# Alpha and phi laid out by partition; in batch 0 ScalarE makes the scales' diagonals and copies both heads' turned exponentials

## The chip, the cores and the metric

The kernel runs on one core of a Trainium2 chip. The metric is device time in microseconds (us) of one execution; lower is better. The core has five instruction streams that run beside each other and wait for one another through semaphores: TensorE (PE in the profile, with its weight loads as PEld), VectorE (DVE), ScalarE (ACT), GpSimd (POOL) and SyncE (SP), which here issues all the DMAs. Each stream works through its instructions strictly in the order in which they were written.

## The reference, cut to what matters

```python
q, k, v: (4, 8, 576, 64)          # batch, heads, positions, width of a head
x = attention(rotate(q), rotate(k), v)            # softmax over 576 keys
x = x.transpose(0, 2, 1, 3).reshape(2304, 512)
h = x @ w_in                                      # (512, 2048)
x = (max(h, 0) + alpha * min(h, 0)) @ w_out       # alpha: (2048,)
logits = x @ phi                                  # (512, 32)
d = softmax(logits, over tokens);  c = softmax(logits, over slots)
slot_input = d.T @ x                              # 32 slots, 4 for each of 8 experts
slot_out[e] = max(slot_input[e] @ w1[e], 0) @ w2[e]
return c @ slot_out                               # (2304, 512)
```

`moe_w_in` and `moe_w_out` arrive as 64-bit floats; the kernel takes each element's two 32-bit words apart itself.

## The kernel before

Attention is cut into 4 batches of 4 pairs of heads. A pair has five rows of query blocks (four of 128 positions for both heads, and a tail). For a row and a head, TensorE makes the scores `st` (L419 in batch 0, L432 in the later ones), VectorE takes the row's maximum (L437), ScalarE the exponentials `e` (L442), VectorE the sum's reciprocal (L449, L450), and GpSimd scales `e` by it (L474). In batch 0 TensorE then turns the scaled exponentials (L495, tile `pt`) and they are copied out of PSUM into `ET`: head 0's by ScalarE (L504), head 1's by VectorE (L506). In batches 1 to 3 the turning is done by VectorE and a way through DRAM instead. `ET` feeds the product with v (L574), which is evacuated into `xt`.

Before that, a pair's q and k are rotated: two multiplications (L322) and an addition (L330 in batch 0, L325 later), on VectorE for the first pair and on GpSimd for all others.

Beside batch 0 the weights are prepared, since the first projection (L735) needs them. `w_in` comes in 8 tiles of 1 MB (`wraw`, L621) and `w_out` transposed in 8 more. VectorE joins each tile's words to 32-bit floats (L643, L645, L647). For a tile of `w_in`, ScalarE and TensorE find its largest value (L655, L229), VectorE makes from it a scale that is a power of two (`sw`, L202 to L206), and GpSimd writes the scaled tile as 16-bit floats (L658). What that rounding left over goes into a second 16-bit tile, in two halves (`split`): GpSimd makes a 128 x 128 matrix with the scale on its diagonal (`dg`, L262), TensorE multiplies the tile by it and subtracts the 16-bit part (L268, L269), and ScalarE copies the rest out (L273). That is 16 halves, and there is one buffer for `dg`. The tiles of `w_out` go into a product with `phi` (L696, L705).

The order of the instructions on every engine is written by a planner (`Plan`): each step (`op`) names its engine, an assumed cost and a due time, and the planner lays the steps out by simulating the engines with these costs. Where a step's engine or cost changes, all that follows may be laid out otherwise. The inputs are prepared on the host by `kernel`: `form` names a function for each array that is laid out anew there.

`alpha` (2048 values) is loaded by L239 into `al`, 128 partitions x 16, and `phi` (512 x 32) by L240 into `phs`, 128 x 4 x 32. Both lie in DRAM in their own order, so `al` is read value by value and `phs` in runs of 32 values.

Of the kernel before, what the change touches and what calls it, by code (L numbers as in the profile page):

```python
# [14 lines left out]
AF = mybir.ActivationFunctionType  # L15
ALU = mybir.AluOpType
# [15 lines left out]
W0, W1, WD, WB, WS, ATT, LEADS, LAG, PRE, ORD = 1.0, 2.2, -6.0, 0.5, 1.0, 3.4, (0.0, 0.3, 0.6, 0.8), 6.0, 9.0, 1.0  # L32
# [130 lines left out]
def attn_moe_softmoe(ctx, tc, qx, kx, vx, w_in, w_out, alpha, phi, w1, w2, tab, msks, w_out_t, out):  # L163
    nc = tc.nc
# [71 lines left out]
        for z, i, d in (("k", 2, -30), ("q", 0, -28))}  # L236
    s_tabs = Slot("tabs")
    msk_op = op(DMA, 450, 15, lambda: nc.sync.dma_start(msk, msks))
    al_op = op(DMA, 900, -3, lambda: nc.sync.dma_start(al, alpha.rearrange("(c p) -> p c", p=128)))  # L239
    phs_op = op(DMA, 450, 9, lambda: nc.sync.dma_start(phs, phi.rearrange("(c p) s -> p c s", p=128)))  # L240
    sel_op = op(DVE, 200, 20, lambda: nc.vector.tensor_reduce(
        sel4[:, 0], idf[:].rearrange("p (g s) -> p s g", s=NS), axis=AX.X, op=ALU.add))
    sel_op = op(DVE, 200, 20, lambda: nc.vector.tensor_copy(
# [11 lines left out]
    def split(due, scale, src, dst, n, cls, dep, uses, after=None):  # L255

        s_d, s_p = Slot("dg"), Slot(cls)
        e = {}

        def diag():  # L260
            e["d"] = wst.tile([128, 128], F32, tag="dg", name="dg", bufs=1)
            nc.gpsimd.tensor_scalar(e["d"], idf, scale(), 1.0, ALU.mult, ALU.mult)  # L262

        def mults():
            ps = ps_m.tile([128, n], F32, tag=cls, name="rest")
            hi = dst(0)
            e["p"] = ps if len(hi.shape) == 2 else ps[:].rearrange("p (r a f) -> p r a f", r=hi.shape[1], a=hi.shape[2])
            nc.tensor.matmul(ps, e["d"], src(), start=True, stop=False)  # L268
            nc.tensor.matmul(ps, neg["t"], hi, start=False, stop=True)  # L269

        o = op(POOL, 470, due, diag, [dep, neg_op], takes=[s_d], uses=[s_d])
        o = op(PE, n * 2.1, due - ATT, mults, [o, dep, after], takes=[s_p], uses=[s_d, s_p] + uses)
        return op(ACT, 595, due, lambda: nc.scalar.activation(dst(1), e["p"], AF.Copy), [o, after], uses=[s_p] + uses)  # L273

# [120 lines left out]
    def row_events(b, p, s, n, pair):  # L395
# [4 lines left out]
        c = {}  # L400
# [69 lines left out]
        for h in heads:  # L470
            def norm(h=h):
                if tail:
                    nc.gpsimd.tensor_scalar(c["e"][:, 1, 0:64], c["e"][:, 0, 512:S], c["mm"][:, 6:7], 1.0, ALU.mult, ALU.mult)
                nc.gpsimd.tensor_scalar(c["e"][:, h], c["e"][:, h], c["mm"][:, 6 + h:7 + h], 1.0, ALU.mult, ALU.mult)  # L474

            o2 = op(POOL, 1200 if tail else 820, n + h + LEADS[1], norm, [o], uses=[s_mm, s_e])
            norms.append(o2)
            if moved:
                def block(h=h):
                    if h == 0:  # L480
                        c["tb"] = att.tile([128, 16, 2, 32], F32, tag="tb", name="tb", bufs=2)
                    nc.vector.transpose(  # L482
                        out=c["tb"][:, :, h].rearrange("p (q m) j -> p q m j", q=4),
                        in_=c["e"][:, h, 64 * h:64 * h + 512].rearrange("p (m q j) -> p q m j", m=4, q=4))

                blocks.append(op(DVE, 760, n + h + LEADS[2], block, [o2] + blocks[-1:], takes=[] if h else [s_tb], uses=[s_e, s_tb]))
                continue
            s_pm = Slot("pm")

            def turn(h=h):  # L490
                if h == 0 and first:
                    open_ET()
                c["pt", h] = ps_m.tile([128, 4, 128], F32, tag="pm", name="pt")
                for i in range(4):
                    nc.tensor.transpose(c["pt", h][:, i], c["e"][:, h, 64 * h + 128 * i:64 * h + 128 * i + 128], idf)  # L495

            def turned(h=h):
                if tail:
                    dst, src = pair["ett"][:, 0:4], c["pt", h]
                else:  # L500
                    dst = pair["ET"][:, 0:2048].rearrange("p (s q m h j) -> p s h m q j", s=2, q=4, m=4, h=2)[:, s % 2, h]
                    src = c["pt", h][:].rearrange("p m (q j) -> p m q j", q=4)
                if h == 0:
                    nc.scalar.activation(dst, src, AF.Copy)  # L504
                else:
                    nc.vector.tensor_copy(dst, src)  # L506

            new = h == 0 and first
            o2 = op(PE, 430, n + h + LEADS[2] - ATT, turn, [o2, pair.get("turn")], takes=[s_pm, s_ET] if new else [s_pm], uses=[s_pm, s_e, s_ET])
            pair.setdefault("turn", o2)  # L510
            evs.append(op(*((DVE, 690) if h else (ACT, 600)), n + h + LEADS[2], turned, [o2] + evs[:1], uses=[s_pm, s_ET]))
        if moved:
            if s % 2 == 0:
                pair["s_sc"] = Slot("sc")
# [991 lines left out]
    return np.ascontiguousarray(w.reshape(E, 2, 4, 128, 2, 256).transpose(0, 4, 1, 3, 2, 5).reshape(E, 2, 2, 128, 1024))  # L1506


def _values(np, v):

    v = v.reshape(B, NP, 2, S, D)
    a = v[:, :, :, :512].reshape(B, NP, 8, 128, D).transpose(0, 1, 3, 2, 4)
    r = v[:, :, :, 512:].reshape(B, NP, 128, 1, D)
    return np.ascontiguousarray(np.concatenate([a, r], 3))
# [27 lines left out]
```

## Time and profile before

| | us |
|---|---|
| median of 3 runs | 661.23 (656.81 to 665.81) |
| the profiled execution | 665.84 |
| its span | 664.1 |
| PE busy | 608.8 |
| DVE busy | 469.7 |
| ACT busy | 354.0 |
| POOL busy | 288.4 |

The profiled execution is the slowest of those shown; its span is the time from the first to the last instruction, and 1.7 us lie around it. Busy times of different engines overlap. PE's busy time includes stretches at half its clock, which the profile gives as the granted clock (1.00 is full).

### The profile page before, as it was taken

The page shows a single profiled execution, that of the slowest core. Times are in us where ns is not written, and L with a number is a line of the kernel's source. Part 1 is how long each engine was busy: PE and PEld are TensorE (multiplying, and loading weights), DVE is VectorE, ACT ScalarE, POOL GpSimd, SP SyncE. Part 2 cuts the span into 40 slices and gives each one's busy share as a digit, 9 for nine tenths or more (in the row PEclk, how much of TensorE's full clock was granted, in tenths as well). Part 3 has the DMA queues.
Part 4 walks back from the last instruction along what each step waited for, and adds up shares of the span by engine and source line. Part 5 has one row for each costly group of instructions (what it writes and reads, how often), then busy time and mean ns, then how long its engine had stood idle before and what let it go on. Part 6 is the DMA issues. An engine that isn't in the chain of part 4 may idle for free.

```text
span 664.1 us, 13901 instructions
## 1 busy us (share of the span) xinstructions
PE 608.8 (92%) x5232; PEld 430.5 (65%) x5232; DVE 469.7 (71%) x1016; ACT 354.0 (53%) x860; POOL 288.4 (43%) x286
## 2 busy tenths in 40 slices
PE   2889868989999999999989999999999999997994
PEld 1546434546887677777867767786877787682352
DVE  5785899786888857896767778677672888843442
ACT  3545545645777766867666775766653232331121
POOL 0697999455557557374644448341330000001000
PEclk9788997977999999999999999999999999997996
DMA  8953363630579987878787885868674993679998
GB/s 287 374 196 97 120 215 127 197 119 0 158 222 243 265 224 217 229 202 229 190 222 198 230 222 158 227 180 205 169 189 120 394 409 123 218 259 372 401 338 284
DMA packets 72674, 146.59 MB, mean 221 GB/s; under 512 B 8352, under 2 KB 37536, under 8 KB 72608
## 3 DMA queue, kind: packets, MB, share of 16 engines
q1 hardware_dynamic: 72608, 145.72, 70.9%
q8 instruction: 41, 0.67, 0.4%
q14 instruction: 25, 0.20, 0.1%
HBM read 108.73 MB, written 29.88 MB: 209 GB/s over the span
## 4 chain that ended last, share of the span: by engine, by line
PE 66%; DMA 11%; DVE 10%; POOL 6%; ACT 3%; SPq 3%; issue 2%; ACTq 0%; DVEq 0%; POOLq 0%
PE ph L735 24%; PE pv L574 12%; PE st L432 6%; DMA ET<-sc 4%; PE pt L754 3%; DMA xw<-in_moe_w_dram 3%; PE lg L772 3%; PE st L419 3%; POOL e L474 2%; PE pt L495 2%; PE po L1316 2%; PE pu L891 2%; DMA sc<-tb 2%; PE rest L268 1%; PE pc L538 1%
## 5 line engine op out<-in xcount | busy, mean ns | idle before, releaser
L474 POOL TENSOR_SCALAR e<-e,mm 128x576 f32<-128x576 f32 x144 | 122.7, 863 | 149.4 <-DVE mm L450 110.0
L735 PEld LDWEIGHTS <-w 128*128 128x128 f16 x1728 | 164.0, 98 | 33.6 <-issue 11.9
L735 PE MATMUL ph<-xt,w 128*128 128x256 f16 x1536 | 183.3, 273 | 1.7 <-DVE g L748 1.0
L437 DVE TENSOR_REDUCE mm<-st 128x1 f32<-128x576 f32 x144 | 106.3, 743 | 28.1 <-PE st L432 22.0
L442 ACT ACTIVATE e<-st,mm 128x576 f32<-128x576 f32 x144 | 106.3, 739 | 31.2 <-DVE mm L437 28.1
L322 POOL TENSOR_TENSOR xn<-xn,tabs 128x576 f32<-128x576 f32 x60 | 90.1, 1515 | 37.6 <-DMA xn<-in_q_dram 26.6
L743 ACT ACTIVATE rl<-ph 128x256 f32<-128x256 f32 x144 | 55.0, 382 | 90.5 <-PE ph L735 90.1
L748 DVE SCALAR_TENSOR_TENSOR g<-rl,oma,ph 128x256 f32<-128x256 f32 x144 | 68.2, 474 | 43.9 <-ACT rl L743 43.4
L432 PE MATMUL st<-ks,qs 128*128 128x288 f32 x384 | 71.7, 314 | 0.3 <-ACT e L442 0.3
L482 DVE STREAM_TRANSPOSE tb<-e 128x512 f32<-128x512 f32 x96 | 66.8, 701 | 5.0 <-POOL e L474 2.6
L574 PE MATMUL pv<-ET,vt 128*64 128x256 f32 x512 | 63.8, 392 | 5.1 <-DMA ET<-sc 2.7
L419 PE MATMUL st<-ks 64*128 64x288 f32 (+1 forms) x168 | 48.1, 507 | 16.1 <-DVE ks L330 11.2
L432 PEld LDWEIGHTS st<-ks,qs 128*128 128x128 f32 x384 | 54.6, 191 | 4.7 <-issue 2.4
L574 PEld LDWEIGHTS pv<-ET,vt 128*64 128x64 f32 x512 | 36.2, 139 | 26.4 <-issue 8.1
L419 PEld LDWEIGHTS st<-ks 64*128 64x128 f32 (+1 forms) x168 | 26.9, 216 | 31.5 <-DVE ks L330 11.2
L759 ACT ACTIVATE gt<-pt 128x512 f32<-128x512 f32 x56 | 33.2, 597 | 13.0 <-PE pt L754 12.2
L495 PE MATMUL pt<-idf,e 128*128 128x128 f32 x192 | 33.5, 310 | 3.3 <-POOL e L474 3.2
L325 POOL TENSOR_TENSOR xn<-xn 128x576 f32<-128x576 f32 x24 | 35.9, 1497 | 0.9
L495 PEld LDWEIGHTS pt<-idf,e 128*128 128x128 f32 x192 | 25.4, 160 | 15.2 <-POOL e L474 7.8
L754 PE MATMUL pt<-idf,g 128*128 128x128 f32 x224 | 33.7, 275 | 0.2
L584 ACT ACTIVATE xt<-pv,vb 128x256 f16<-128x256 f32 x32 | 15.1, 473 | 33.9 <-PE pv L574 33.8
L952 POOL MEMSET edt<- 128x256 f32 x1 | 0.3, 313 | 75.4 <-DVE lp L916 75.4
(182 smaller groups left out, 909.8 us busy)
## 6 DMA issues: line engine op xcount, KB each, us to landing
sc<-tb SPq DMA_DIRECT2D x48, 512.0 KB, 4.5
ET<-sc SPq DMA_DIRECT2D x96, 256.0 KB, 5.6
xw<-in_moe_w_dram SPq DMA_DIRECT2D x42, 512.0 KB, 9.9
xn<-in_k_dram SPq DMA_DIRECT2D x16, 576.0 KB, 4.8
xn<-in_q_dram SPq DMA_DIRECT2D x16, 576.0 KB, 5.5
wraw<-in_moe_w_in_dram SPq DMA_DIRECT2D x8, 1024.0 KB, 8.0
wraw<-in_w_out_t_dram SPq DMA_DIRECT2D x8, 1024.0 KB, 5.3
wor<-in_moe_w_out_dram SPq DMA_DIRECT2D x16, 512.0 KB, 11.0
```

Source lines behind the costliest of these rows:

```text
L322: eng.tensor_tensor(e["x"][:, w], e["x"][:, w], tabs[:, (0 if z == "q" else 2) + w], ALU.mult)
L419: nc.tensor.matmul(st[to, j, at:at + w], x, k[rows, z:z + w], start=True, stop=True)
L432: nc.tensor.matmul(st[:, j, 0:288], r["q"][:, 768 * h + 128 * s:768 * h + 128 * s + 128].bitcast(F32R), r["k"][:, a, h, ks].bitcast(F32R), ...
L437: nc.vector.tensor_reduce(c["mm"][:, h:h + 1], c["st", h][:, :, 0:288], axis=AX.XY, op=ALU.max, negate=True)
L442: nc.scalar.activation(c["e"][:, h].rearrange("p (a n) -> p a n", a=2), c["st", h][:, :, 0:288], AF.Exp, bias=c["mm"][:, h:h + 1], accum_o ...
L474: nc.gpsimd.tensor_scalar(c["e"][:, h], c["e"][:, h], c["mm"][:, 6 + h:7 + h], 1.0, ALU.mult, ALU.mult)
L482: nc.vector.transpose(out=c["tb"][:, :, h].rearrange("p (q m) j -> p q m j", q=4), in_=c["e"][:, h, 64 * h:64 * h + 512].rearrange("p (m q ...
L495: nc.tensor.transpose(c["pt", h][:, i], c["e"][:, h, 64 * h + 128 * i:64 * h + 128 * i + 128], idf)
L574: nc.tensor.matmul(pv[r], v[k, 4 * h + i if i < 4 else 8], x, start=(i == 0), stop=(i == 4))
L735: nc.tensor.matmul(ph, wi[j][:, wp, kc, 128 * fo:128 * fo + 128], xt[:, xp, kc, :], start=(n == 0), stop=(n == 3 * KC - 1),)
L743: nc.scalar.activation(c["r"], c["ph"], AF.Relu, scale=-1.0)
L748: nc.vector.scalar_tensor_tensor(blk["g", j][:, fo, :], c["r"], oma[:, f:f + 1], c["ph"], ALU.mult, ALU.add)
```

## The change

`alpha` and `phi` are laid out on the host as the tiles want them (`_columns`: index within a chunk first, then the chunk), so that each partition reads one run: 64 bytes of `alpha`, 512 bytes of `phi`. The step that makes `dg` moves from GpSimd (planned at 470 ns) to ScalarE (planned at 250 ns), as an activation with a scale per partition. In batch 0, head 1's copy into `ET` moves from VectorE (planned at 690 ns) to ScalarE (600 ns), which has head 0's already.

```diff
@@ attn_moe_softmoe
-    al_op = op(DMA, 900, -3, lambda: nc.sync.dma_start(al, alpha.rearrange("(c p) -> p c", p=128)))
-    phs_op = op(DMA, 450, 9, lambda: nc.sync.dma_start(phs, phi.rearrange("(c p) s -> p c s", p=128)))
+    al_op = op(DMA, 900, -3, lambda: nc.sync.dma_start(al, alpha))
+    phs_op = op(DMA, 450, 9, lambda: nc.sync.dma_start(phs, phi))
@@ split
-            nc.gpsimd.tensor_scalar(e["d"], idf, scale(), 1.0, ALU.mult, ALU.mult)
+            nc.scalar.activation(e["d"], idf, AF.Copy, scale=scale())
-        o = op(POOL, 470, due, diag, [dep, neg_op], takes=[s_d], uses=[s_d])
+        o = op(ACT, 250, due, diag, [dep, neg_op], takes=[s_d], uses=[s_d])
@@ row_events
-                if h == 0:
+                if h == 0 or not b:
                     nc.scalar.activation(dst, src, AF.Copy)
                 else:
                     nc.vector.tensor_copy(dst, src)
-            evs.append(op(*((DVE, 690) if h else (ACT, 600)), n + h + LEADS[2], turned, [o2] + evs[:1], uses=[s_pm, s_ET]))
+            evs.append(op(*((DVE, 690) if h and b else (ACT, 600)), n + h + LEADS[2], turned, [o2] + evs[:1], uses=[s_pm, s_ET]))
+def _columns(np, x):
+    return np.ascontiguousarray(x.reshape((-1, 128) + x.shape[1:]).swapaxes(0, 1))
@@ kernel
-    form = {"q": _keys, "k": _keys, "v": _values, "moe2_w2": _second}
+    form = {"q": _keys, "k": _keys, "v": _values, "moe2_w2": _second, "moe_alpha": _columns, "moe2_phi": _columns}
```

The planner lays out all of batch 0 anew. Three places follow, with - for before and + for after.

GpSimd, from the first scaled tile of `w_in` (`w_177`) on, beside the rotation of the second pair (`xn`, `ks`):

```order
 L658 TENSOR_SCALAR w_177<-w_177,sw 128x4x256
 L322 TENSOR_TENSOR xn<-xn,tabs 128x576
-L262 TENSOR_SCALAR dg<-idf,sw 128x128
+L474 TENSOR_SCALAR e<-e,mm 128x576
 L330 TENSOR_TENSOR ks<-xn 128x576
+L322 TENSOR_TENSOR xn<-xn,tabs 128x576
 L474 TENSOR_SCALAR e<-e,mm 128x576
-L322 TENSOR_TENSOR xn<-xn,tabs 128x576
-L262 TENSOR_SCALAR dg<-idf,sw 128x128
 L322 TENSOR_TENSOR xn<-xn,tabs 128x576
 L474 TENSOR_SCALAR e<-e,mm 128x576
 L330 TENSOR_TENSOR ks<-xn 128x576
```

Both diagonals of the first tile are gone from this stream, and a scaling of exponentials stands in the first one's place.

ScalarE at the same place, where the second row's exponentials and the next tile's largest value (`w_242`) are made:

```order
 L442 ACTIVATE e,mm<-st,mm 128x576
-L542 ACTIVATE ec<-pc 128x128
-L442 ACTIVATE e,mm<-st,mm 128x576 x2
+L504 ACTIVATE ET<-pt 128x4x4x32
+L542 ACTIVATE ec<-pc 128x128
+L442 ACTIVATE e,mm<-st,mm 128x576
+L262 ACTIVATE dg<-idf,sw 128x128
 L655 ACTIVATE w_242,mws<-w_242 128x4x256
 L442 ACTIVATE e,mm<-st,mm 128x576 x2
+L262 ACTIVATE dg<-idf,sw 128x128
 L273 ACTIVATE w_177<-rest 128x2x256
 L504 ACTIVATE ET<-pt 128x4x4x32
```

Head 1's copy and both diagonals have come in between the exponentials.

VectorE at the same place, between the first tile's scale (`sw`, L205 and L206) and the second tile's words:

```order
 L643 TENSOR_SCALAR w_242<-wraw 128x8x128
 L205 TENSOR_SCALAR inv_w<-mws 128x1
-L506 COPY ET<-pt 128x4x4x32
+L645 SCALAR_TENSOR_TENSOR w_242<-wraw,w_242 128x8x128
 L206 RECIPROCAL sw<-inv_w 128x1
 L449 TENSOR_SCALAR mm<-mm 128x2
 L437 TENSOR_REDUCE mm<-st 128x1
 L450 RECIPROCAL mm<-mm 128x2
-L645 SCALAR_TENSOR_TENSOR w_242<-wraw,w_242 128x8x128
-L437 TENSOR_REDUCE mm<-st 128x1
 L647 SCALAR_TENSOR_TENSOR w_242<-wraw,w_242 128x8x128
```

The copy is gone, and the second tile's L645 has moved up ahead of the scale's last step.

The order of the first DMAs on SyncE is the same up to the load of the masks (L238); only the forms of `al` and `phs` differ.

## Rows read from the trace of the kernel before

**Rows 1.** Busy us (and count) of each engine, granted clock, DMA share, GB/s, by stretches.

```profile
0.00:24.00 24.00, 10.85 (x37) 7.40 (x37) 14.10 (x40) 9.27 (x21) 2.47 (x9) 1.00 0.93 315
24.00:122.00 98.00, 83.95 (x417) 47.25 (x419) 78.94 (x135) 50.54 (x117) 92.02 (x75) 0.84 0.51 174
84.00:110.00 26.00, 19.82 (x105) 11.17 (x107) 25.42 (x35) 11.91 (x29) 25.87 (x19) 0.80 0.66 216
122.00:166.00 44.00, 39.09 (x247) 23.90 (x247) 32.59 (x55) 22.65 (x54) 22.50 (x18) 0.81 0.31 95
166.00:600.00 434.00, 424.22 (x4019) 327.75 (x4011) 320.13 (x707) 260.04 (x648) 169.57 (x182) 1.00 0.75 219
600.00:664.00 64.00, 50.70 (x518) 24.16 (x518) 23.98 (x82) 11.45 (x24) 1.84 (x2) 0.86 0.96 353
25.00:35.00 10.00, 8.91 (x21) 4.86 (x23) 7.56 (x14) 5.49 (x13) 10.00 (x9) 0.52 1.01 353
140.00:157.00 17.00, 13.77 (x50) 7.57 (x52) 12.07 (x21) 7.00 (x18) 12.57 (x9) 0.54 0.11 36
```

**Rows 2.** Timeline of SyncE's issues: start us, us, engine, line, operation.

```profile
4.91 0.45 SPq L239 DMA_DIRECT2D al<-in_moe_alpha_dram  x1
5.94 7.62 SPq L291 DMA_DIRECT2D vt<-in_v_dram  x1
13.60 0.98 SPq L621 DMA_DIRECT2D wraw<-in_moe_w_in_dram  x2
14.63 0.50 SPq L319 DMA_DIRECT2D xn<-in_k_dram  x1
```

**Rows 3.** Busy time by short stretches, columns as in rows 1.

```profile
10.00:13.00 3.00, 1.82 (x8) 1.20 (x8) 1.09 (x2) 1.11 (x4) 0.00 (x0) 1.00 1.07 375
13.00:16.00 3.00, 1.30 (x4) 0.68 (x3) 2.50 (x4) 1.71 (x5) 0.00 (x0) 1.00 0.89 92
```

**Rows 4.** DMA issues between 14.6 and 14.7 us: KB, us to landing.

```profile
xn<-in_k_dram SPq DMA_DIRECT2D x1, 576.0 KB, 9.5
```

**Rows 5.** Timeline of GpSimd, from 18 to 31 us; idle time before in brackets.

```profile
18.25 1.47 POOL L474 TENSOR_SCALAR e<-e,mm 128x576 f32<-128x576 f32 x2 [16.55 <-DVE mm L450]
24.30 1.40 POOL L322 TENSOR_TENSOR xn<-xn,tabs 128x576 f32<-128x576 f32 x1 [4.58 <-DVE mm L449]
25.68 2.09 POOL L658 TENSOR_SCALAR w<-w,sw 128x1024 f16<-128x1024 f32 x1
```

**Rows 6.** The diagonals' line: ns min/median/max, and who waited for it (us, times).

```profile
L262 POOL TENSOR_SCALAR dg<-idf,sw x16: 366/811/1347, 30.1 to 114.1; 128x128 f32<-128x128 f32 x16
...
  PEld rest L268: 7.4, 8
  PE rest L268: 4.3, 5
```

**Rows 7.** GpSimd's instructions by line, 24 to 122 us: busy us, mean ns.

```profile
L262 POOL TENSOR_SCALAR dg<-idf,sw 128x128 f32<-128x128 f32 x16 | 12.7, 793 | 0.8 <-PE rest L268 0.8
```

**Rows 8.** Chain of waits from 0 to 165 us: shares by line, then pieces (start, us).

```profile
by line: PE st L419 10.4%; POOL e L474 10.0%; PE pv L574 9.4%; PE pt L495 6.8%; PE rest L268 5.5%; DMA vt<-in_v_dram 4.9%; POOL xn L322 4.1%; DMA xn<-in_q_dram 4.0%; POOL dg L262 3.8%; issue 3.3%; DVE w L647 2.9%; DVE mm L437 2.8%; DVE wx L
...
33.92 0.35 POOL dg L262
...
84.22 0.69 DVE ET L506
...
114.10 1.35 POOL dg L262
```

**Rows 9.** Lines by themselves, to 165 us (L506, L504 whole): ns min/median/max.

```profile
L506 DVE COPY ET<-pt x16: 671/691/693, 23.4 to 165.1; 128x512 f32<-128x512 f32 x16
L504 ACT ACTIVATE ET<-pt x16: 588/597/600, 20.9 to 164.7; 128x512 f32<-128x512 f32 x16
L542 ACT ACTIVATE ec<-pc x15: 267/277/278, 22.3 to 162.4; 128x128 f32<-128x128 f32 x15
L584 ACT ACTIVATE xt<-pv,vb x7: 454/474/475, 43.4 to 159.5; 128x256 f16<-128x256 f32 x7
L743 ACT ACTIVATE rl<-ph x1: 384/384/384, 164.2 to 164.2; 128x256 f32<-128x256 f32 x1
```

## Prediction

> **What bounds the kernel now.** First the busy times by stretches [rows 1]. From 166 to 600 us PE is busy 424.2 of 434 us at full clock: there the kernel is TensorE's work and little else. The last 64 us have a DMA share of 0.96; those loads of expert weights start when attention's buffers come free, so they move along with what goes before. What the change touches lies ahead of that, in batch 0, and the stretches differ. Up to 24 us the chip waits for loads: DMA share 0.93, PE busy 10.9 us. From 24 to 122 us GpSimd is busy 92.0 of 98 us and is the fullest engine; VectorE follows with 78.9, and between 84 and 110 us it has only 0.6 us free of 26. PE is busy 84.0 us at a mean clock of 0.84, ScalarE 50.5. From 122 to 166 us no engine is full. So the question is by how much earlier batch 0 and the weights are done; after 166 us PE's work is the same and has next to no idle time in which a lead could be lost, so I count a microsecond won before 166 us as one won at the end.
>
> Next come the diagonals [rows 6, 7]: 16 instructions, 12.7 us on GpSimd, between 366 and 1347 ns each for the same shape, and TensorE's `rest` matmuls waited for them 4.3 us, their weight loads 7.4 us. Then the chain of waits to 165 us [rows 8]: `dg` holds 3.8% of it, 6.3 us, in seven pieces of 0.35 to 1.35 us; head 1's copy on VectorE stands in it three times before 165 us, at up to 0.69 us. Last the start of the SyncE stream [rows 2]: the issue behind `al` is held for 7.62 us, and two weight tiles and the second pair's k wait behind it.
>
> **The change part by part.** The sum is made against the profiled execution, 665.84 us. That is 4.6 us above the median of the runs shown, 661.23, so at the end I scale by 661.23 / 665.84 = 0.993.
>
> *Alpha and phi.* From 13 to 16 us the DMA engines are busy (share 0.89) but move 92 GB/s, against 375 in the three microseconds before [rows 3]. `al` is what is in the queue then: 2048 values of 4 bytes. The stretch moved what would have taken 3 x 92 / 375 = 0.7 us, so 2.3 us were lost, and everything queued behind came that much later, among it the second pair's k: issued at 14.63 us, landed 9.5 us later at 24.1 [rows 4]. GpSimd's first rotation starts right then, at 24.30, after 4.58 us without work [rows 5]. (The row names VectorE as releaser, but the landing fits.) Bounds: 0, if what GpSimd does next sets the pace, since L658, which waits for the first tile's scale from VectorE, follows only at 25.68 us; and 7.6 us, the whole hold of the queue, if the loads come earlier by all of it. The DMA was at full rate for most of the hold, so I stay near the lost throughput: **-2.3 us**. `phi` goes from 512 runs to 128, in the same queue; I give it nothing, its cover being the loads around it.
>
> *The diagonals.* GpSimd loses 16 instructions, 12.7 us of its 92.0. ScalarE gains 16. No row shows this one there; nearest are a 128 x 128 copy at 0.277 us (L542), with a fixed scale, and the pair L584 and L743, 128 x 256 with a scale per partition at 0.474 and without at 0.384 [rows 9]. So 0.277 + 0.090 = 0.37 us, or 5.9 us in all. ScalarE has 47.5 us free between 24 and 122 us [rows 1], which covers it as long as the instruction isn't waiting itself. On the chain, 6.3 us of GpSimd go, and if ScalarE's instruction stands in each of the seven places 7 x 0.37 = 2.6 us come: **-3.7 us**. The upper bound is the full 12.7 us, if GpSimd's fullness is what sets the stretch's length, not only the pieces that the chain names. The lower bound is a loss: `dg` has one buffer, and its second half must wait for TensorE's use of the first. On GpSimd that held up rotations; on ScalarE the next exponentials are queued behind it (in the new order an L655 and two L442 behind the first, `rest`'s evacuation behind the second), and scores, turning and v's product wait for these.
>
> *Head 1's copies.* 16 x 0.691 = 11.1 us leave VectorE and 16 x 0.597 = 9.6 us come to ScalarE [rows 9]; the copy already had to follow head 0's, so nothing that ran side by side is put in line. In the chain's three places that gives 3 x 0.09 = 0.3 us at best. The rest is what VectorE does sooner: the first copy (23.4 us) stood ahead of the first tile's scale, and two copies lie between 84 and 110 us, where VectorE has no gap, 2 x 0.69 = 1.4 us. Where it has gaps I take nothing: the cover is its 19 us of idle time between 24 and 122 us. **-1.6 us**, between 0 and the 11.1.
>
> *Clock.* TensorE ran at half of its 2.4 GHz in four stretches, of which the first (25 to 35 us) and the longest (140 to 157 us) stand in the rows [rows 1]; in each, PE had been short of work just before. The new order deals these anew. Losing the longest would give 17 x 0.46 = 8 us, another like it costs as much. I take 0 and put it into the range.
>
> Sum: -2.3 - 3.7 - 1.6 = -7.6 us, so 658.2 against the profile and x 0.993 = **653.6 us** against the median. I say 653.5.
>
> **The rivals.**
>
> *GpSimd sets the length of the stretch.* Then all 12.7 us count: -2.3 - 12.7 - 1.6 = -16.6, 649.2, or **644.7 us**. For it: 92.0 of 98 us busy. Against: VectorE has no gap from 84 to 110 us, and PE is busy 84 of these 98 us.
>
> *The waits stay.* The same diagonal takes 366 or 1347 ns [rows 6]; the long ones start while VectorE runs L645 or L647. If so, 16 x 0.43 = 6.8 us of the 12.7 aren't the diagonal's work but a wait beside VectorE, and the next GpSimd instruction inherits it. On the chain 7 x 0.37 = 2.6 us go and 2.6 come, net 0: -3.9 us, 661.9, or **657.3 us**. For it: the spread. Against: other GpSimd instructions have the same waits and aren't made more numerous. The Trainium skill (SBUF — State Buffer, "Who interferes with whom") states this as a rule: VectorE and GpSimd share a pair of ports that one instruction holds for its whole length, while ScalarE never waits on anyone. By that rule the trace's spread is expected, and this rival is the right price of the diagonals.
>
> *ScalarE becomes the one that is waited for* (the other side). Its stream is in order, and each diagonal can stop it until L658 is through (up to 2.09 us [rows 5]) or the buffer is free. If the 11.7 us that TensorE waited for diagonals [rows 6] become waits of ScalarE with exponentials behind them, and all reach the chain, it is +11.7 - 2.3 - 1.6 = +7.8, 673.6, or **669.0 us**. It becomes a loss from the point where such waits on the chain exceed the 3.9 us that the other two parts save. Against: even with the new work, 50.5 + 5.9 + 6.0 (ten copies) of 98 us, ScalarE has over a third of the stretch idle, so many of its waits fall into time that it has.
>
> *The queue isn't held by `al`.* The ring may be full of the megabytes ahead of it. Then only -5.3 us remain: 660.5, or 655.9 us. Against: the 92 GB/s at full busy share.
>
> **How the numbers follow.** Forecast 0.42, GpSimd sets the length 0.24, the waits stay 0.21, ScalarE waited for 0.08, the queue 0.05. The range, 643 to 663, takes the first three and the last whole with some of the clock's play on either side; it leaves out most of the ScalarE case and the far ends of the clock. Two per cent, about what a measurement of this kernel can tell from no change (its runs span 1.4%), is 13 us: faster than 648.0 is the GpSimd case and a little of the forecast with a clock stretch gone, 0.28; slower than 674.5 needs the ScalarE case with one clock stretch more, 0.03; within it 0.69.
>
> **What would show it.** SyncE's issue after `al` takes under 1 us and no stretch before 20 us falls under 300 GB/s at full share; GpSimd's first rotation starts at 21 to 23 us. L262 stands on ScalarE at 0.3 to 0.45 us, 16 times, and the waits of `rest` for it are under half of 11.7 us. GpSimd's busy time falls by 10 to 13 us (by some 6 where the waits stay: then the means of L322 and L474 rise). L506 is gone and L504 counts 32 in batch 0. The first L735 starts some 8 us earlier than before (162.7 us). I am wrong if batch 0 ends earlier and the end doesn't follow, if ScalarE's idle time before L262 is over 6 us, or if a half-clock stretch appears or goes and covers the rest.

## The result, and the profile after

The changed kernel is slower: median 669.32 us over 20 runs (662.12 to 674.70), the kernel before 662.25 us over 20 runs beside it; the ratio is 1.0088 with a 95% interval of 1.0064 to 1.0113, some 5.8 us. The ratio leaves out runs more than 1.5% above their kernel's fastest, six of the changed kernel's 20 and none of before's, so it is smaller than that of the medians (1.0107). I had forecast 653.5 us, in a range of 643 to 663. The profiled execution after took 672.49 us (span 670.7), above its median, as that of before was above its own (665.84 against 662.25). A second profile of the very same instructions (run lag_8, below) has a span of 661.6; what is said of the changed kernel after 200 us holds in both.

The start of SyncE's stream in the changed kernel; start us, us, engine, line. It answers to [rows 2]:

```profile
4.98 0.47 SPq L239 DMA_DIRECT2D al<-in_moe_alpha_dram  x1
6.29 0.33 SPq L291 DMA_DIRECT2D vt<-in_v_dram  x1
7.72 1.83 SPq L621 DMA_DIRECT2D wraw<-in_moe_w_in_dram  x2
9.92 1.35 SPq L319 DMA_DIRECT2D xn<-in_k_dram  x1
```

The issue behind `al` takes 0.33 us in place of 7.62, and the second pair's k is issued at 9.92 us in place of 14.63. GpSimd at the same place, as in [rows 5]:

```profile
22.02 1.83 POOL L322 TENSOR_TENSOR xn<-xn,tabs 128x576 f32<-128x576 f32 x1 [1.97 <-DMA xn<-in_k_dram]
25.18 1.12 POOL L658 TENSOR_SCALAR w<-w,sw 128x1024 f16<-128x1024 f32 x1 [1.32 <-DVE mm L449]
```

The first rotation starts 2.28 us earlier (24.30 before), and now the row names the load as its releaser. But L658 starts only 0.50 us earlier (25.68): it waits for VectorE.

The diagonals in the changed kernel, as in [rows 6]:

```profile
L262 ACT ACTIVATE dg<-idf,sw x16: 389/400/417, 26.5 to 103.2; 128x128 f32<-128x128 f32 x16
...
  PE rest L268: 2.7, 2
...
  PEld rest L268: 0.8, 1
...
  PE rest L268: 0.3, 1
```

ScalarE was idle for 2.7 us before them (the first of the three waits), and `rest` waited 0.3 and 0.8 us for them, against 4.3 and 7.4 before. Up to here it went as forecast.

Busy us (and count) by stretches, of the changed kernel, in columns as in [rows 1]; in the engines' columns the first is PE:

```profile
13.00:16.00 3.00, 1.30 (x5) 0.48 (x2) 2.16 (x4) 1.36 (x4) 0.00 (x0) 1.00 1.06 375
24.00:122.00 98.00, 85.64 (x470) 47.78 (x468) 84.56 (x135) 61.95 (x148) 84.54 (x61) 0.93 0.53 178
122.00:166.00 44.00, 40.82 (x258) 25.26 (x256) 28.91 (x55) 26.26 (x61) 22.79 (x20) 0.77 0.31 96
166.00:600.00 434.00, 416.34 (x3917) 320.68 (x3916) 317.80 (x686) 254.37 (x631) 166.84 (x179) 0.99 0.73 215
0.00:200.00 200.00, 170.86 (x1064) 109.05 (x1066) 152.72 (x276) 122.59 (x291) 129.45 (x108) 0.91 0.54 180
200.00:300.00 100.00, 89.02 (x765) 66.27 (x765) 72.27 (x159) 63.05 (x153) 54.38 (x55) 0.98 0.76 207
```

The same view of the kernel before, for the stretches that [rows 1] don't cut there:

```profile
0.00:200.00 200.00, 167.78 (x1017) 106.68 (x1019) 154.08 (x292) 108.64 (x254) 135.53 (x122) 0.88 0.54 176
200.00:300.00 100.00, 97.78 (x860) 75.28 (x857) 78.51 (x174) 70.66 (x174) 61.55 (x62) 1.00 0.83 231
```

PE's count of matmuls shows the story, since both kernels issue the same ones (a rough measure: they differ in length). At 200 us the changed kernel has done 47 more (1064 against 1017); at the 8.6 per us that the kernel before does from there on, it is 5.5 us ahead. From 200 to 300 us it does 765 in place of 860 and loses 95 / 8.6 = 11.0 us. So it stands 5.5 us behind at 300 us, and the spans differ by 6.6. A lead at 200 us was there, and it was lost in batch 1, where the change moves no work at all: it only lets the planner write another order.

How large that lead was, one execution can't tell. The same instructions did 1064 matmuls by 200 us here and 1094 in run lag_8. Nor does it show what the moved work gives: with the new layout alone, in before's order, 1063 were done (run layout_only), and from 24 to 122 us the mean granted clock was 0.84 before, 0.91 with the layout alone and 0.93 here. The loss from 200 to 300 us is far steadier; before's order with the layout alone and with the work moved, then the changed order a second time and with the old engines:

```profile
200.00:300.00 100.00, 97.69 (x874) 75.02 (x873) 77.66 (x174) 71.46 (x176) 58.50 (x60) 1.00 0.85 234
200.00:300.00 100.00, 97.37 (x866) 74.83 (x866) 76.86 (x172) 70.69 (x175) 58.34 (x59) 1.00 0.84 232
200.00:300.00 100.00, 89.60 (x768) 67.76 (x767) 72.50 (x163) 65.64 (x160) 54.23 (x55) 0.98 0.73 204
200.00:300.00 100.00, 90.05 (x774) 67.46 (x773) 70.97 (x158) 63.69 (x155) 54.41 (x55) 0.97 0.79 214
```

What the loss looks like: projection matmuls (L735) alone, in the changed kernel and then in the kernel before, PE and PEld:

```profile
264.00:287.00 23.00, 0.11 (x2) 0.00 (x0) 0.93 0.77 229
```

```profile
265.00:287.00 22.00, 7.52 (x65) 5.87 (x62) 1.00 0.90 223
```

For 23 us TensorE has next to no projection to fill in: all its matmuls together take 18.3 of these 23 us, 141 in number, where the kernel before has 22.7 us and 205 from 264 to 287 us. The chain of waits of the changed kernel there (start us, us):

```profile
279.65 5.39 DMA sc<-tb
285.04 0.02 SPq L528
...
286.45 7.23 DMA ET<-sc
293.68 0.14 issue
293.82 2.53 PE pv L574 x20
```

The product with v hangs on the turned exponentials' way through DRAM, 12.6 us for its two transfers. The transfers themselves took about as long before (medians 6.4 and 5.7 us from 166 to 300 us). And GpSimd's waits from 166 to 300 us (us in total, times, longest), first before, then after:

```profile
POOL e L474 <- DVE mm L450: 17.8, 9, 5.3
```

```profile
POOL e L474 <- DVE mm L450: 40.0, 12, 6.3
```

Scaling waits for the row sums more than twice as long. That the scores come late in TensorE's order, and all that follows them with it, would fit this, but no run shows it.

### The profile page after: what moved, and what is told of

Its sections match the earlier page's. It is cut to its first block, busy times and chain, and to the rows that moved or that the text cites. A ratio compares the mean times of both kernels' runs of the same rounds, so it can differ in the third digit from the quotient of the medians.

```text
span 670.7 us, 13900 instructions
## 1 busy us (share of the span) xinstructions
PE 609.4 (91%) x5232; PEld 429.6 (64%) x5232; DVE 472.1 (70%) x1000; ACT 366.6 (55%) x892; POOL 280.3 (42%) x270
## 4 chain that ended last, share of the span: by engine, by line
PE 64%; DMA 11%; DVE 11%; POOL 5%; ACT 3%; SPq 2%; issue 2%; DVEq 0%; ACTq 0%
PE ph L735 23%; PE pv L574 12%; PE st L432 5%; DMA ET<-sc 5%; PE st L419 4%; DMA xw<-in_moe_w_dram 3%; PE pt L754 3%; PE lg L772 2%; PE pt L495 2%; PE pu L891 2%; PE po L1316 2%; DMA sc<-tb 2%; POOL xn L322 2%; POOL e L474 2%; DVE mm L437 1%
## 5 line engine op out<-in xcount | busy, mean ns | idle before, releaser
L735 PEld LDWEIGHTS <-w 128*128 128x128 f16 x1728 | 164.1, 98 | 35.5 <-issue 14.6
L474 POOL TENSOR_SCALAR e<-e,mm 128x576 f32<-128x576 f32 x144 | 119.1, 837 | 161.1 <-DVE mm L450 120.1
L735 PE MATMUL ph<-xt,w 128*128 128x256 f16 x1536 | 182.9, 273 | 1.6 <-DVE g L748 1.5
L322 POOL TENSOR_TENSOR xn<-xn,tabs 128x576 f32<-128x576 f32 x60 | 91.8, 1546 | 37.2 <-DMA xn<-in_q_dram 18.9
L419 PE MATMUL st<-ks 64*128 64x288 f32 (+1 forms) x168 | 48.0, 503 | 15.9 <-DVE ks L330 11.5
L419 PEld LDWEIGHTS st<-ks 64*128 64x128 f32 (+1 forms) x168 | 26.7, 213 | 29.9 <-DVE ks L330 11.5
L495 PEld LDWEIGHTS pt<-idf,e 128*128 128x128 f32 x192 | 24.6, 158 | 19.6 <-POOL e L474 12.7
L449 DVE TENSOR_SCALAR mm<-mm 128x2 f32<-128x2 f32 (+1 forms) x80 | 26.3, 330 | 12.2 <-ACT e L442 11.8
```

Source lines behind the costliest of these rows:

```text
L322: eng.tensor_tensor(e["x"][:, w], e["x"][:, w], tabs[:, (0 if z == "q" else 2) + w], ALU.mult)
L419: nc.tensor.matmul(st[to, j, at:at + w], x, k[rows, z:z + w], start=True, stop=True)
L735: nc.tensor.matmul(ph, wi[j][:, wp, kc, 128 * fo:128 * fo + 128], xt[:, xp, kc, :], start=(n == 0), stop=(n == 3 * KC - 1),)
```

## The experiments

All ratios are to the kernel before on the same chip, with 95% intervals. The last two columns are PE's matmuls up to 200 us and from 200 to 300 us, of one profiled execution each (a few records may be missing).

| run | ratio | median us | to 200 | 200 to 300 |
|---|---|---|---|---|
| before | 1 | 662.25 | 1017 | 860 |
| the change | 1.0088 (1.0064 to 1.0113) | 669.32 | 1064 | 765 |
| layout_only | 0.9965 (0.9939 to 0.9990) | 659.76 | 1063 | 874 |
| moved_old_order | 0.9962 (0.9932 to 0.9991) | 659.38 | 1045 | 866 |
| new_order_old_engines | 1.0187 (1.0142 to 1.0231) | 673.79 | 1022 | 774 |
| lag_8 | 1.0092 (1.0054 to 1.0130) | 668.70 | 1094 | 768 |
| fetch_first | 1.0461 (1.0413 to 1.0508) | 691.84 | 1082 | 730 |
| batch0_new_rest_old | 1.0084 (1.0053 to 1.0115) | 667.25 | 997 | 873 |
| batch0_old_rest_new | 1.0222 (1.0180 to 1.0264) | 677.31 | 948 | 786 |
| layout_cost_480 | 0.9982 (0.9954 to 1.0011) | 660.78 | 1056 | 881 |
| projections_later | 1.1633 (1.1585 to 1.1681) | 768.28 | 977 | 676 |
| diagonals_only | 1.0137 (1.0094 to 1.0180) | 670.79 | 1014 | 815 |
| copies_only | 1.0008 (0.9971 to 1.0044) | 662.61 | 1075 | 812 |
| diagonal_cost_400 | 0.9835 (0.9795 to 0.9875) | 650.00 | 1147 | 876 |
| diagonal_cost_410 | 1.0039 (1.0012 to 1.0066) | 662.64 | 1096 | 800 |
| diagonal_cost_330 | 0.9940 (0.9910 to 0.9969) | 655.79 | 1093 | 868 |
| diagonal_cost_450 | 0.9986 (0.9954 to 1.0019) | 658.31 | 1065 | 882 |
| cost_400_old_engines | 1.0020 (0.9993 to 1.0047) | 661.27 | 1017 | 860 |
| block1_later_4 | 1.0443 (1.0407 to 1.0480) | 690.43 | 1071 | 616 |
| block1_later_10 | 1.0383 (1.0342 to 1.0425) | 686.23 | 1084 | 641 |

### The parts, and order apart from engines

layout_only: the kernel before with alpha and phi laid out anew; the order is word for word before's.

> Only alpha and phi laid out by partition; every instruction stands in the order of the kernel before. Two theories of the 6 us that the change lost. ORDER: the moved work saves time in batch 0 (the last score matmul of batch 0 came at 152 us and not 161), and the loss is in the order that the planner wrote for the rest, where TensorE uses up its projection matmuls early and waits between 200 and 300 us (89.0 us busy against 97.8). ENGINES: ScalarE's new work itself costs, by its waits, whatever the order. Both expect of the layout alone 0 to 4 us less than before (about 658 to 662), since it touches neither; the hold of 7.62 us in SyncE's stream is gone and the stretch 13 to 16 us moves over 350 GB/s.

It gains 0.35%, 2.3 us (0.7 to 4.0).

moved_old_order: all of the change is executed, but the planner is told before's engines and costs, and so writes before's order.

```diff
-        o = op(ACT, 250, due, diag, [dep, neg_op], takes=[s_d], uses=[s_d])
+        o = op(POOL, 470, due, diag, [dep, neg_op], takes=[s_d], uses=[s_d])
-            evs.append(op(*((DVE, 690) if h and b else (ACT, 600)), n + h + LEADS[2], turned, [o2] + evs[:1], uses=[s_pm, s_ET]))
+            evs.append(op(*((DVE, 690) if h else (ACT, 600)), n + h + LEADS[2], turned, [o2] + evs[:1], uses=[s_pm, s_ET]))
```

> The changed kernel's three parts, but the planner is told the engines and costs of before, so that every stream keeps its order of before, with the diagonals and copies put into ScalarE's stream where the plan of before had them. ORDER: 4 to 10 us faster than before (652 to 658), TensorE's busy time from 200 to 300 us at 96 us or more. ENGINES: 3 to 9 us slower than before (665 to 671), and ScalarE waits over 6 us ahead of the diagonals.

0.9962, the same as the layout alone: in before's order the moved work is worth nothing, give or take 2.6 us. And yet TensorE's `rest` waited 2.4 us for diagonals in place of layout_only's 15.4. GpSimd's busy time from 24 to 122 us fell from layout_only's 92.17 to

```profile
24.00:122.00 98.00, 84.00 (x463) 48.25 (x460) 81.52 (x130) 63.42 (x151) 84.75 (x61) 0.91 0.52 171
122.00:166.00 44.00, 40.44 (x247) 25.22 (x240) 29.93 (x53) 24.08 (x57) 21.91 (x18) 0.77 0.29 91
```

84.75 us, but the matmuls done by 200 us didn't rise (1045 against 1063), batch 0's last scores (L419) came no earlier (156.7 us against 155.7), and from 122 to 166 us the granted clock was 0.77 against layout_only's 0.84. What TensorE no longer waited for there, it waited for elsewhere.

new_order_old_engines: the reverse. The changed kernel's order, but GpSimd makes the diagonals and VectorE copies head 1's exponentials.

```diff
-            nc.scalar.activation(e["d"], idf, AF.Copy, scale=scale())
+            nc.gpsimd.tensor_scalar(e["d"], idf, scale(), 1.0, ALU.mult, ALU.mult)
-                if h == 0 or not b:
+                if h == 0:
```

> The changed kernel's order on TensorE and SyncE to the row, and on the others but for the moved work: the planner is told that ScalarE makes the diagonals and head 1's copies, but GpSimd and VectorE do it as before; alpha and phi are laid out anew. ORDER: 6 to 14 us slower than before (668 to 676), with TensorE under 92 us busy from 200 to 300 us. ENGINES: as before or a little faster (658 to 663).

1.0187: in this order the moved work is worth 1.0% (0.5 to 1.5), and the order itself is what costs. (This order was planned for the work on ScalarE, before's for it on GpSimd and VectorE; how much of the 1.0% comes from that, no run shows.) `rest` waited 11.6 and 15.6 us for diagonals here, against 0.3 and 0.8 with ScalarE.

lag_8: the constant `LAG`, a due time of the projections, 8.0 in place of 6.0.

> The changed kernel, with the first projection's due times moved by two half-rows (LAG 8.0 for 6.0), so that the planner keeps more of its matmuls for batch 1. ORDER, if it is the early use of these matmuls: TensorE's busy time from 200 to 300 us rises from 89 to 94 us or more and the time falls by 4 to 9 us against the changed kernel (660 to 665). ENGINES: no change against the changed kernel (667 to 671). If it falls into neither, the idle time is not a matter of when these matmuls are due.

The planner wrote the same order with it, instruction for instruction, so the run tells nothing about lag. It is a second measurement of the changed kernel: 1.0092, and 768 matmuls from 200 to 300 us.

### Which part of the order

Three kernels have the changed kernel's engines and layout. In fetch_first SyncE alone differs: a stacking of k (L363) that stood up to three DMA steps ahead of a fetch of exponentials (L528) is issued behind it.

```diff
-    for o in plan.order():
+    for i, o in enumerate(dmas):          # SyncE's steps in the changed kernel's order
+        if o.back:
+            for x in dmas[max(0, i - 3):i]:
+                if x.stack:
+                    rank[id(x)] = rank[id(o)] + 0.5
```

> The changed kernel with its own order on PE, VectorE, ScalarE and GpSimd; only SyncE's stream is touched: a stacking of k (L363, four DMAs) that stood up to three DMA steps ahead of a fetch of turned exponentials (L528) is issued behind that fetch. Theory A, the loss after 200 us is head-of-line waiting in SyncE's queue (fetches held behind stackings that wait for TensorE): ratio to before 0.998 to 1.004, PE busy from 200 to 300 us 94 us or more (89.0 in the changed kernel), v's product (L574) waiting for ET there under 1.5 us (4.2). Theory B, TensorE's own sequence in batch 1 (projection matmuls spent early, attention late) is the cause: ratio 1.006 to 1.013 as the changed kernel, PE busy 88 to 91.

As a remedy this failed: 1.0461. It didn't test theory A cleanly, for the wait that it was to remove stayed: v's product waited 3.8 us for `ET` from 200 to 300 us (4.2 in the changed kernel, under 1.5 expected). PE's busy time there fell to 86.4 us. Another wait came in, for exponentials that GpSimd scaled late, 5.9 us from 200 to 300 us and from 300 to 500 us

```profile
PE pc L538 <- POOL e L474: 9.6, 2, 5.8
```

The two hybrids put steps of batch 0 and the weights by one order and those of batches 1 to 3 by the other (`merged` writes the steps by their rank, each as soon as the steps and buffers that it needs are there):

```diff
-    for o in plan.order():
+    for o in merged(plan, lambda o: (new if part[id(o)] else old)[id(o)]):    # batch0_new_rest_old
+    for o in merged(plan, lambda o: (old if part[id(o)] else new)[id(o)]):    # batch0_old_rest_new
```

> The changed kernel's engines and layout. The steps of batch 0 and of the weights stand among themselves as in the changed kernel's order, those of batches 1 to 3 as in the order of the kernel before. Theory A/B alike, the loss lies in the order of batches 1 to 3: ratio 0.988 to 0.997, PE busy from 200 to 300 us 96 or more. If the first 166 us' new order is what costs (a rival, C: it hands over to batch 1 with other work left): ratio 1.005 to 1.013, PE busy from 200 to 300 us under 92.

> The reverse: batch 0 and the weights in the order of the kernel before, batches 1 to 3 in the changed kernel's, engines and layout as changed. If the loss lies in the order of batches 1 to 3: ratio 1.005 to 1.015, PE busy from 200 to 300 us under 92. If in that of batch 0 (C): ratio 0.993 to 1.000, PE busy 96 or more.

The pace from 200 to 300 us goes with the order of batches 1 to 3: 873 matmuls with before's, 786 with the changed one. But the totals missed. Where the two orders meet, batch 0 itself was slowed: from 122 to 166 us, first batch0_new_rest_old,

```profile
122.00:166.00 44.00, 38.27 (x201) 22.78 (x199) 24.45 (x43) 22.73 (x55) 20.55 (x18) 0.73 0.27 88
```

then batch0_old_rest_new,

```profile
122.00:166.00 44.00, 37.38 (x191) 21.52 (x191) 26.71 (x45) 19.23 (x45) 19.28 (x16) 0.69 0.24 82
```

201 and 191 matmuls against 258 in the changed kernel. In these two mixtures half of one order didn't fit half of another.

layout_cost_480: layout_only, but the planner is told 480 ns for a diagonal on GpSimd in place of 470.

> A control: only alpha and phi laid out anew, diagonals on GpSimd and copies on VectorE as before, but the planner is told 480 ns for a diagonal in place of 470, so that it lays out everything from 50 us on afresh with the same work on the same engines. If re-laying alone moves the time by about as much as this change did, the ratio is outside 0.992 to 1.001 (layout alone was 0.9965), either way, with another PE busy time in 200 to 500 us than 97 to 98. If the changed kernel's loss comes from what was moved and not from a fresh order: 0.993 to 1.000.

0.9982: the same work, another order from 50 us on, and no loss. So a fresh order isn't a loss as such.

### Alone, and with other costs told

diagonals_only and copies_only each have the layout and one of the two moves, planned as executed. diagonal_cost_400 is the whole change with one number altered:

```diff
-        o = op(ACT, 250, due, diag, [dep, neg_op], takes=[s_d], uses=[s_d])
+        o = op(ACT, 400, due, diag, [dep, neg_op], takes=[s_d], uses=[s_d])
```

> Layout and diagonals on ScalarE, planned with them; head 1's copies on VectorE as before. In its order 54 and 84 scores of batch 1 stand ahead of the 128th and the 192nd projection matmul (before 54 and 92, changed kernel 50 and 66). Theory B: near before's pace after 200 us, PE busy from 200 to 300 us 95 or more, ratio 0.988 to 0.998. If the loss belongs to the diagonals on ScalarE as such: ratio 1.004 to 1.012.

> Layout and head 1's copies on ScalarE, planned with them; the diagonals on GpSimd as before. In its order 46 and 66 scores of batch 1 stand ahead of the 128th and the 192nd projection matmul, as in the changed kernel. Theory B: slow after 200 us, PE busy from 200 to 300 us under 92, ratio 1.004 to 1.016. If not: 0.990 to 0.999 with 95 or more.

> The whole change, but the planner is told 400 ns for a diagonal on ScalarE, which is what the traces show, in place of 250. In its order 54 and 74 scores stand ahead of the 128th and the 192nd projection matmul, as in the control with 480 ns on GpSimd, which kept its pace. Theory B: PE busy from 200 to 300 us 95 or more, ratio 0.988 to 0.998: the change then gains. If the moved work itself costs: 1.004 to 1.012.

The last gains 1.65% (1.25 to 2.05), a median of 650.0 us: the fastest version here. The two parts alone are 1.0137 and 1.0008, with PE busy 95.0 and 94.0 us from 200 to 300 us, which neither theory had. So the count of scores ahead of the projections, on which I had forecast them, isn't the measure: diagonals_only had the better count and the worse time. The profile of diagonal_cost_400 by stretches:

```profile
122.00:166.00 44.00, 40.34 (x341) 28.69 (x340) 37.74 (x71) 31.87 (x77) 30.78 (x26) 1.00 0.43 141
0.00:200.00 200.00, 167.41 (x1147) 110.92 (x1148) 159.81 (x298) 128.21 (x308) 141.35 (x116) 0.97 0.60 194
200.00:300.00 100.00, 97.50 (x876) 74.76 (x875) 77.88 (x169) 72.83 (x176) 55.38 (x57) 1.00 0.81 223
```

It is 130 matmuls ahead of before at 200 us and keeps before's pace from 200 to 300 us. Up to 122 us it has done 506, as the changed kernel has (36 + 470 in both); from 122 to 166 us it does 341 against 258, at a granted clock of 1.00 against 0.77. So its lead over the changed kernel arises where this order has no half-clock stretch. Of the 83 matmuls some 30 lie within what one order does from run to run: lag_8, with the changed kernel's instructions, did 288 there at 0.88.

400 ns is what the diagonal takes (389/400/417), so a truer price might have made the better order. The next runs ask that, with the same line at 410, 330 and 450 ns, and with 400 ns but the old engines (the edit of new_order_old_engines).

> The whole change, the planner told 410 ns for a diagonal, 10 ns more than in the version that gained 1.65%. In this order 66 scores of batch 1 stand ahead of the 192nd projection matmul, as in the changed kernel (74 at 400 ns). Theory P, a price near the real one (389 to 417 ns) makes a good order: ratio 0.980 to 0.990. Theory L, each fresh order is a draw, and a step of 10 ns draws anew: ratio anywhere from 0.98 to 1.02, and at most by chance near 0.9835; PE busy from 200 to 300 us tells where.

> The whole change, the planner told 330 ns. In this order the projections stand among batch 1's scores as in the kernel before (54 and 92 scores ahead of the 128th and 192nd), only batch 0 is laid out afresh. If a lead won in batch 0 is kept where batch 1 keeps before's pattern: PE busy from 200 to 300 us 96 or more and a ratio of 0.982 to 0.994. Theory P alone: worse than at 400 ns, 0.992 to 1.01.

> The whole change, the planner told 450 ns; 54 and 92 scores ahead of the 128th and 192nd projection matmul, as before. Theory P: 0.982 to 0.992, little worse than at 400 ns. Theory L: a draw of its own, with PE busy from 200 to 300 us 96 or more if the place of the projections tells the pace.

> The order of the version planned with 400 ns, but GpSimd makes the diagonals and VectorE copies head 1's exponentials, as before. With new_order_old_engines (1.0187, beside 1.0088 with the work moved) this tells what the moved work is worth in a second order. If it is worth the same 1%: ratio 0.991 to 0.998. If in a good order it is worth what I forecast for both parts, 5.3 us: 0.989 to 0.994. If the order does it all: 0.980 to 0.987.

At 410 ns the time is 1.0039, 2% above that at 400 ns, where theory P wanted 0.980 to 0.990. (Its profiled execution took 669.41 us, 6.8 above its median.) So a true price isn't what did it: a step of 10 ns draws a new order. At 330 ns, where the projections stand among the scores as before, the time came as expected. Of the whole change there are five such orders, at 250, 330, 400, 410 and 450 ns: 1.0088, 0.9940, 0.9835, 1.0039 and 0.9986, a mean of 0.9978, about what the layout alone gives (0.9965). In the order at 400 ns the moved work is worth 1.85% (1.4 to 2.3; 1.0020 with the old engines), more than any of the three cases expected; in that at 250 ns 1.0%, in before's nothing.

### Why batch 1 is slow in some orders

In the changed kernel, lag_8, new_order_old_engines, diagonals_only, copies_only and diagonal_cost_410, all of them slow from 200 to 300 us, there are some 20 us between 250 and 290 us with at most 15 projection matmuls; in the kernels that do 860 or more matmuls from 200 to 300 us, any 20 us between 250 and 290 us have at least 24. Theory B: projections spent early leave TensorE without filler. First with all projections set where before's order has them, then, since that mixes two whole orders, with only the second block's projections set 4 and 10 attention steps later in the changed kernel's own order:

```diff
-    for o in plan.order():
+    for i, o in enumerate(seq):           # the changed kernel's order
+        rank[id(o)] = (i, 0, 0)
+        if id(o) in late:                 # second block's projections
+            rank[id(o)] = (steps[bisect.bisect(steps, i) - 1 + 4], 1, i)
```

> The changed kernel with its engines, its layout and its own order of all attention and weight steps; only the steps of the projections and experts (L735 and what follows from it) are set among TensorE's attention steps where the order of the kernel before has them: at the 192nd projection matmul 92 scores of batch 1 are behind it in place of 66. Theory B, the new order spends the projections early and leaves TensorE without filler while attention's way through DRAM runs: PE busy from 200 to 300 us 95 or more (89.0 in the changed kernel), no gap of several us at 270 to 285, ratio to before 0.990 to 0.999. Theory A', attention's own new order in batch 1 (k's stacking, fetches, SyncE) is slow whatever lies beside it: PE busy 88 to 92, ratio 1.004 to 1.015.

> The changed kernel with its own order throughout, except the projection steps of the second block of tokens (projection matmuls 193 to 384 and what follows from them): each is set four of TensorE's attention steps later, so that at the 256th projection matmul 112 scores of batch 1 are behind it (changed kernel 104, before 130). The slow orders all have 20 to 25 us with next to no projection matmul between 250 and 290 us. Theory B, projections spent early leave TensorE without filler and keep attention behind: PE busy from 200 to 300 us 91 to 94 (89.0), ratio 1.000 to 1.006. Theory A', attention's own order limits: 87 to 90, ratio 1.007 to 1.015.

> The same with ten attention steps: 134 scores behind the 256th projection matmul, 176 behind the 384th (before 130 and 172). Theory B: PE busy from 200 to 300 us 94 or more, no stretch of 20 us without projections, ratio 0.992 to 1.002. Theory A': scores and products with v placed ahead of the projections wait for their inputs, PE busy 84 to 90, ratio 1.007 to 1.03.

All three are far slower, by more than either theory gave. In block1_later_10 that hole is filled, as this row of L735 alone shows,

```profile
264.00:287.00 23.00, 8.28 (x64) 6.31 (x62) 0.93 0.73 199
```

with 64 projections in place of 2, and yet PE is idle for 20 us of the 100:

```profile
200.00:300.00 100.00, 80.02 (x641) 57.78 (x642) 62.15 (x137) 56.54 (x136) 48.32 (x50) 0.94 0.70 193
```

Its waits there are spread over many places, none of which reaches 3 us in all. But the hole was moved more than filled: from 200 to 222 us this kernel has 11 projection matmuls (the changed kernel 72), with PE busy 17.9 of 22 us (21.3 in the changed kernel), and from 287 to 303 us 7. In block1_later_4 likewise 6 from 224 to 242 and 11 from 287 to 307 us. So these two don't decide on theory B. Against it speaks projections_later, which has at least 20 in any 20 us from 200 to 300 us and is the slowest of all, but it mixes two orders. What is left: the hole is a mark of the slow orders, and whether it is their cause stays open.

## Why the prediction was wrong

**The step that failed** is the one that carried batch 0's gain to the end: "after 166 us PE's work is the same and has next to no idle time in which a lead could be lost, so I count a microsecond won before 166 us as one won at the end". The work is the same; its order isn't. PE's 424.2 busy of 434 us [rows 1] was a property of before's order in batch 1, and I read it as one of the kernel. The change re-laid that order too, and PE's busy time there became 416.3. I had written that the planner lays all of batch 0 anew, and looked no further than batch 0. The prediction named this outcome as a sign of its being wrong (batch 0 ends earlier and the end doesn't follow): batch 0's last scores start at 152.1 us in place of 161.4, 155.7 with the layout alone. A second step failed beside it, the price of the moved work: in before's order, where nothing was lost after 166 us, the whole change gained 2.5 us (0.9962) and not 7.6. Of the 13.4 us between forecast and result (-7.6 and +5.8) the order so accounts for 8.3 and that price for 5.1.

**Alpha and phi, -2.3.** Right: layout_only has -2.3 us (-4.0 to -0.7). 13 to 16 us now moves 375 GB/s, where [rows 3] had 92.

**The diagonals, -3.7, and the copies, -1.6.** Together -5.3. There is no one value: 0 in before's order, 0.0187 - 0.0088 = 1.0% or 6.6 us in the changed one, 1.85% or 12.2 us in that at 400 ns. I priced them from the waits on one chain in one order, and in that very order most of those waits went and the end didn't follow. The unit cost, 0.37 us, was measured at 0.40.

**Clock, 0 with 8 us either way.** Batch 0's longest stretch stayed (140 to 157 us at 0.58, [rows 1] had 0.54); in the order at 400 ns it went (1.00), and the lead of 83 matmuls there is 9.7 us. Taking lag_8's 288 for the changed order, it is 53 and 6.2 us. So the term was sized about rightly, but the clock isn't all that a new order deals.

**The rivals.** ScalarE isn't the one waited for: 2.7 us idle before the diagonals, 1.1 us waited for them. I had the loss on this side alone, with the wrong mechanism. "GpSimd sets the length" isn't borne out: its busy time from 24 to 122 us fell by 7.5 us in the changed kernel and by 7.4 in before's order, where the end didn't move. For "the waits stay" I had named a fall of some 6 us, against 10 to 13 if not; 7.5 is nearer to it. Of the two means that were to rise only that of L322 did (1640 to 1686 ns), while L474's fell (1182 to 1080); but L330's rose from 1564 to 2052 ns and those of L658's two groups from 1363 and 1118 to 1614 and 1595, 5.8 us more for the same count. So some 5 of the 12.7 us came back in other instructions, and this rival's price for the diagonals, nothing, is what before's order gave (0 within 2.6 us); in the two orders planned for the change it was too low. "The queue isn't held by `al`" is refuted by the 0.33 us. The sign that I gave for the handover, the first L735 some 8 us earlier, failed as well: 163.9 us against 162.7 (160.6 in lag_8, the same order).

**Shown and open.** Shown: the loss lies in batch 1's pace and goes with its order, on whichever engine the moved work runs; one number in the planner draws another order, and with it from 0.9835 to 1.0088 of the time. Open: which waits inside a slow order make it slow. Edits on two guesses, one on SyncE's stream and one on the projections, made it slower without deciding either guess.

## What to carry to other kernels

Where a planner writes the order, a change of one cost can redraw everything behind it, also where no work is moved: forecast the mean of the draws and a range as wide as they are, which here five values of one cost showed to be 2.5%. Before judging such a change, run it in the old order and run it in a few fresh ones; keep the best order, not the first. A full engine's lack of idle time belongs to the order as much as to the work. And mending a fine-grained order over five streams by hand is hard: the four edits tried here (fetches first, and three shifts of the projections) cost the changed kernel a further 3 to 15%. A wait that goes from one engine is no time won until the end shows it: in before's order `rest` waited 13 us less and the kernel was no faster.

## What was unexpected of the hardware

A diagonal of 128 x 128 with a scale per partition takes ScalarE 400 ns, where the copy of the same shape takes 277 [rows 9]: 123 ns more, not the 90 that the 256-wide pair gave. (That copy also reads PSUM and the diagonal SBUF, so the 123 ns aren't the scale's alone.) In one and the same order the diagonals took 389 to 417 ns on ScalarE and, in new_order_old_engines, 365 to 1409 ns on GpSimd:

```profile
L262 POOL TENSOR_SCALAR dg<-idf,sw x16: 365/372/1409, 28.4 to 108.9; 128x128 f32<-128x128 f32 x16
```

The spread is gone with the engine. Each of the four diagonals above 1.3 us there ends about 0.24 us after an L645 or L647 of VectorE that had started before it. The Trainium skill (SBUF — State Buffer, "Who interferes with whom") gives the reason why it may: GpSimd shares one pair of ports with VectorE, of two instructions that need this pair the first holds it for its whole length while the other blocks, and ScalarE waits for nobody. This pair of runs agrees, with 365 to 1409 ns on GpSimd and 389 to 417 ns on ScalarE.
